# Two fill products between row and key scores in every step, and an earlier query fetch, in a kernel of attention and a Fourier layer

## The chip, the cores and the metric

One core of a Trainium2 chip. The metric is device time in microseconds for one execution, the median of several. Engines: PE is TensorE (PEld its weight loads), DVE VectorE, ACT ScalarE, POOL GpSimd, SP SyncE, which issues nearly all DMAs. PSUM holds what TensorE writes.

## The reference

Two independent layers whose outputs stand side by side; everything is fp32.

```
# A: attention, x [2048, 1024], 32 heads of 32, one k and v for all heads
q = x @ wq;  k = x @ wk;  v = x @ wv
p = softmax(q_h @ k.T * 32**-0.5)          # for each head h: 2048 x 2048
a = concat_h(p @ v) @ wo
# B: Fourier layer, xB [2048, 1024]
re = xB @ Wd_re.T;  im = xB @ Wd_im.T
b = Ws_re @ re - Ws_im @ im
out = concat([a, b], axis=-1)              # [2048, 2048]
```

## The kernel before

**Units and steps.** Attention is cut into 32 units: 4 blocks of 512 queries by 8 groups of four heads. A unit takes 32 steps (`SU`), and each step handles two different units at two stages. The first is a *row step* `score_step(s)`: `scores(s)` makes the scores of 128 queries by 1024 keys with two products into a PSUM tile `pss` (two buffers); VectorE takes the row maximum (`TENSOR_REDUCE nm<-pss`, 1024 of them); `row_sums(s)`, which is emitted one step later, lets ScalarE take the exponential in place and sum it. The sums and maxima give the log-sum of each row, which `lse_1` to `lse_4` write into two spare rows of the query tile `qst`. The second is a *key step* n = s - 52 (`SU + LEAD`): `key_scores(n)` makes the transposed scores of 128 keys by 1024 queries with two products into `pst` (one buffer of two PSUM banks), with the log-sum already subtracted, and `key_exp(n)` lets ScalarE take the exponential into an SBUF tile `p` (15 buffers).

**Bursts.** In steps 15 and 31 of a unit (`LASTS`) `pv` multiplies the exponentials of eight chunks of keys with v: 64 matmuls of 32 columns, four heads side by side, into a bank `psb`. This is the burst. `key_exp` of that step is emitted after its first chunk.

**Fills.** All other matmuls of the two layers (query and output projections and the Fourier layer, each fp32 product as three fp32r products of high and low parts, and with seven products for eight by Strassen's scheme) are a list of groups of 24 or 12 products, which accumulate in one of two PSUM banks (`ps_b`). `take(n)` emits the next n of them; I call them fills. `pos["fill"]` counts them, and a planner (`Line`, `pump`, `at`) issues loads, casts and stores by that count. When a group is complete, `post` reads its bank, on VectorE as a rule. There are 5328 fills ahead of the last groups, 408 of them before step 0.

**Spread of the fills.** `goal(n)` says how many fills should be done by step n; `level(n)` takes the rest up to the goal of the next burst, divided by the steps that are left, rounded. In a burst step it takes none, but `pv` first calls `aside`, which takes 0 to 5 fills so that the open group is at least six products old or complete. TensorE's order in a step was: row scores, key scores, then all fills of the step (or `aside`'s and the burst).

**Query tiles.** `qst` has three buffers. `open_unit(u + 1)` is emitted in row step 26 of unit u (`SU - 6`), six steps ahead of its first row scores: three DMAs from `qh_d` and `ql_d` and, from the fourth tile on, one that clears two rows. All go through SP's queue, in order with the other loads and stores.

Each engine runs its instructions in the order in which the program emits them. Nearly all instructions have one line in the profile (L79), since the class `Ordered` emits them; groups are told apart by their tiles: `pss<-kst,qst` is a row score, `pst<-qst,kst` a key score, `psb<-rh,mh` and the like a fill, `psb<-p,v` the burst.

Of the kernel before, what the change touches and what calls it, by code (L numbers as in the profile page):

```python
# [101 lines left out]
def tile_kernel(ctx: ExitStack, tc, xT, wq, wkv, wo, xbT, wT, cT, out):  # L102
# [51 lines left out]
    class Line:  # L154
# [24 lines left out]
        def pump(self):  # L179
            for k in range(4):  # L180
                while self.may(k) and self.items[self.n[k]].due - self.lead[k] <= pos["fill"]:
                    self.step(k)
# [94 lines left out]
    def add(gs):  # L277

        for g in gs:
            i0 = g.at = end[0]  # L280
            end[0] += g.n
            if groups and g.set[0] is not groups[-1].set[0]:
                prev["set"] = prev["this"]
                prev["this"] = i0
            for c, it in enumerate(g.right):
                if it.need is None:
                    it.need = i0 + 3 * c
                    p0 = min(prev["set"], i0 - it.back)
                    it.due = min(it.need, p0 + (i0 - p0) * (g.first + c + 1) // (len(g.set) * len(g.right))) - it.ahead
                    RL.items.append(it)  # L290
                it.last = i0 + 3 * c + 2
            for c, it in enumerate(g.left):
                if it.need is None:
                    it.need = it.due = i0 + 12 * c
                    ML.items.append(it)
                it.last = i0 + 12 * c + 11
            for it in g.ys:
                it.due = i0 + g.n
                ylist.append(it)
            groups.append(g)  # L300
# [14 lines left out]
    def at(p, f):  # L315
        k = len(later)
        while k and later[k - 1][0] > p:
            k -= 1
        later.insert(k, (p, f))

    def run_later():
        while later and later[0][0] <= pos["fill"]:
            later.pop(0)[1]()
# [29 lines left out]
    def bank(name, open_=False):  # L353

        while held:
            held.pop(0)()
        b = 1 - cur["bank"] if cur["bank"] is not None else int(used[1] < used[0])
        cur["at"] += 1
        used[b] = cur["at"]
        if open_:  # L360
            cur["bank"] = b
        return ps_b[b].tile([P, W], F32, name=name)
# [10 lines left out]
    def product(g, ps, j):  # L373
        c, w = divmod(j, 3)
        l, r = g.left[c // 4], g.right[c]
        a = (l.lo if w == 2 else l.hi)[:, c % 4]
        te.matmul(ps[:g.rows], a, r.lo if w == 1 else r.hi, start=j == 0, stop=j == g.n - 1)

    def take(n):
        for _ in range(n):  # L380
            if cur["group"] >= len(groups):
                return
            g = groups[cur["group"]]
            j = pos["fill"] - g.at
            if j == 0:
                cur["ps"] = bank("psb", True)
            if j % 3 == 0:
                RL.force(g.right[j // 3])
            if j % 12 == 0:
                ML.force(g.left[j // 12])  # L390
            product(g, cur["ps"], j)
            pos["fill"] += 1
            if j == g.n - 1:
                cur["group"] += 1
                assert all(hasattr(it, "done") for it in g.ys)
                g.post(cur["ps"])
                cur["at"] += 1
                used[cur["bank"]] = cur["at"]
                cur["bank"] = None
                if g.ys:  # L400
                    at(pos["fill"] + 2 * BEHIND + 5, lambda n=len(g.ys): yused.__setitem__(0, yused[0] + n))
            pump()
            run_later()
# [174 lines left out]
    def wo_set(e):  # L578
        return [Item([(lambda g=g: wo[g * P:(g + 1) * P, e * W:(e + 1) * W], 1)]) for g in range(NG)]
# [143 lines left out]
    units = [(b, g) for b in range(NQ) for g in range(NG)]  # L723
    SU = 32
# [5 lines left out]
    def open_unit(u):  # L730
        b, g = units[u]
        assert ("q", b, g) in ready
        if u < 3:
            rows.append(qsp.tile([P, 4, W], F32R, name=f"qst{u}"))
            gp.memset(rows[u][96:P].bitcast(F32), 0.0)
        q = rows[u % 3]
        if u >= 3:
            move(sp, q[96:98].rearrange("p a b -> p (a b)"), kst[98:100])
        for r, src in enumerate((qh_d, ql_d, qh_d)):
            move(sp, q[r * DH:(r + 1) * DH], src[b][g].rearrange("(h d) c -> d h c", d=DH))  # L740
        qst[u] = q
        nm[u] = sm.tile([P, 10, NC], F32, name="nm")

    def scores(s):
        u, r = divmod(s, SU)
        i, j = divmod(r, 2)
        h, t = divmod(i, 4)
        ps = ps_s.tile([P, 2 * W], F32, name="pss")
        for a in range(2):
            k0 = (2 * j + a) * W  # L750
            te.matmul(ps[:, a * W:(a + 1) * W], qst[u][:, h, t * P:(t + 1) * P], kst[:, k0:k0 + W], start=True, stop=True)
        dve.tensor_reduce(nm[u][:, j, i:i + 1], ps, axis=AX.X, op=ALU.max, negate=True)
        pend[s] = ps

    def row_sums(s):
        if s not in pend:
            return
        ps = pend.pop(s)
        u, r = divmod(s, SU)
        i, j = divmod(r, 2)  # L760
        act.activation(ps, ps, AF.Exp, bias=nm[u][:, j, i:i + 1], accum_out=nm[u][:, 8 + j, i:i + 1])
# [24 lines left out]
    def lse_3(u):  # L786
        pm = ps_s.tile([P, 2 * W], F32, name="pss")
        te.transpose(pm[:3 * NC, :P], nm[u][:, 3:6].rearrange("p a b -> p (a b)"), ident)
        mt = sm.tile([3 * NC, P], F32, name="mt")
        dve.tensor_copy(mt, pm[:3 * NC, :P])  # L790
        lse[u] = mt
# [7 lines left out]
    def inverse(u):  # L799
        rb[u] = onp.tile([P, W], F32, name="rb")  # L800
        for h in range(4):
            r = r_d[u][4 * h:4 * h + 4].rearrange("t c -> (t c)")
            sp.dma_start(rb[u][h * DH:(h + 1) * DH], r.unsqueeze(0).to_broadcast([DH, W]))

    def key_scores(n):
        u, r = divmod(n, SU)
        c, hp_ = divmod(r, 2)
        ps = ps_t.tile([P, 2, W], F32, name="pst")
        for a in range(2):
            te.matmul(ps[:, a], kst[:, c * P:(c + 1) * P], qst[u][:, 2 * hp_ + a], start=True, stop=True)  # L810
        return ps

    def key_exp(n, ps):
        u, r = divmod(n, SU)
        c, hp_ = divmod(r, 2)
        pt[u, c, hp_] = pp.tile([P, 2, W], F32, name="p")
        act.activation(pt[u, c, hp_], ps, AF.Exp)
# [49 lines left out]
    def score_step(s):  # L867

        if s < total:
            u, r = divmod(s, SU)  # L870
            if r == SU - 6 and u + 1 < len(units):
                open_unit(u + 1)
        if SU <= s < SU * (len(units) + 1) and s % SU == TURN:
            row_sums(s - 1)
            lse_3((s - SU) // SU)
        if s < total:
            scores(s)
        row_sums(s - 1)
        u, e = divmod(s - SU, SU)
        if 0 <= u < len(units):  # L880
            for f in LSE.get(e, ()):
                f(u)
# [37 lines left out]
    for s in range(SU + LEAD):  # L920
        score_step(s)
        take(6)
# [9 lines left out]
    def goal(n):  # L932
        return PRO + (FILL - PRO - LAST - MORE * (total - QUIET)) * n // total + MORE * max(n - QUIET, 0)


    def level(n):
        r = n % SU
        if r in LASTS:
            return
        more = min(e for e in LASTS if e > r) - r  # L940
        left = goal(n + more + 1) - pos["fill"]
        take(round(left / more))

    for n in range(total):
        u, r = divmod(n, SU)
        if n == total - 12:
            w1 = wo_set(1)
            add([o_group(NQ - 1, t, e, ws) for e, ws in ((0, w0), (1, w1)) for t in range(4)])
        score_step(n + SU + LEAD)
        if ends:  # L950
            ends.pop(0)()
        ps = key_scores(n)
        if r == 16:
            inverse(u)
        if r in LASTS:
            pv(u, LASTS.index(r), lambda: key_exp(n, ps))
        else:
            key_exp(n, ps)
        level(n)


    last = groups[len(groups) - 8:]
# [73 lines left out]
```

## Time and profile before

| | |
|---|---|
| median of 3 runs | 2704.43 us (2704.22 to 2705.95) |
| profiled execution, its own time | 2704.65 us |
| its span, first to last instruction | 2702.9 us |
| mean granted TensorE clock | 0.999 |
| PE busy | 2691.3 us, 13820 matmuls |
| ACT busy | 2128.3 us, 79% |
| POOL busy | 1736.4 us, 64% |
| DVE busy | 1569.6 us, 58% |

Matmuls are pipelined: one is shown with about 0.39 us, though the next starts sooner, so TensorE's pace is read from the distance of starts and not from busy time. A wait counts only where it makes a hole in the stream of the engine that sets the end.

### The profile page before, as it was taken

To read this page: it belongs to the slowest core of one execution; us is meant where nothing else is said; L and a number is where in the kernel's file an instruction comes from. 1 tells how busy PE (TensorE), PEld (TensorE's weight loads), DVE (VectorE), ACT (ScalarE), POOL (GpSimd) and SP (SyncE) were. 2 spreads that over 40 slices of the span, in tenths; PEclk is the share of its full clock that TensorE was granted. 3 is DMA by queue.
4 is the path that set the end of the run, shared out by engine and by line. 5 is a ranking of instruction groups with operands and counts; after the bars stand their busy time and mean duration, and the time that the engine had idled before them with its cause. 6 is when DMAs were issued, how large, how long until landed. Compare 5 with 4: busy or idle time off the path is not lost.

```text
span 2702.9 us, 40398 instructions
## 1 busy us (share of the span) xinstructions
PE 2691.3 (100%) x13820; PEld 1922.0 (71%) x13820; DVE 1569.6 (58%) x1794; ACT 2128.3 (79%) x3130; POOL 1736.4 (64%) x1712
## 2 busy tenths in 40 slices
PE   9999999999999999999999999999999999999999
PEld 6876776677667677677776776677677677667767
DVE  5866666666666666555655556665565556556300
ACT  3688888888888878888888887788898888788641
POOL 4754525777557548766556775566797898866741
PEclk9999999999999999999999999999999999999999
DMA  8543335887687565564444678874675666644565
GB/s 275 184 141 119 122 108 187 291 285 238 228 299 272 189 228 188 172 195 137 145 152 152 198 245 286 292 242 137 219 225 167 210 195 179 193 140 152 184 211 186
DMA packets 316930, 538.24 MB, mean 199 GB/s; under 512 B 35962, under 2 KB 63354, under 8 KB 316666
## 3 DMA queue, kind: packets, MB, share of 16 engines
q1 hardware_dynamic: 315572, 533.69, 61.1%
q8 instruction: 109, 1.79, 0.3%
q10 hardware_dynamic: 1152, 1.97, 0.2%
q14 instruction: 97, 0.79, 0.1%
HBM read 395.58 MB, written 138.15 MB: 197 GB/s over the span
## 4 chain that ended last, share of the span: by engine, by line
PE 68%; DMA 1%; issue 0%; ACT 0%; POOL 0%; DVE 0%; SPq 0%; POOLq 0%; DVEq 0%; ACTq 0%
PE psb L79 42%; PE pst L79 13%; PE pss L79 12%; DMA m<-o 1%; DMA y<-c 0%; DMA out_dram<-y 0%; DMA qst<-qh 0%; ACT pss L79 0%; ACT p L79 0%; DMA c<-y 0%; POOL ov L79 0%; POOL ml L79 0%; DVE nm L79 0%; SPq L79 0%; POOL m L79 0%
## 5 line engine op out<-in xcount | busy, mean ns | idle before, releaser
L79 DVE TENSOR_REDUCE nm<-pss 128x1 f32<-128x1024 f32 x1024 | 1252.4, 1223 | 530.3 <-PE pss L79 529.3
L79 ACT ACTIVATE p<-pst 128x1024 f32<-128x1024 f32 x1026 | 1059.1, 1032 | 451.3 <-PE pst L79 362.7
L79 ACT ACTIVATE pss<-pss,nm 128x1024 f32<-128x1024 f32 x1024 | 1118.0, 1092 | 55.7 <-DVE nm L79 54.2
L79 PE MATMUL psb<-rh,mh 128*128 128x512 f32 x1790 | 699.5, 391 | 0.1
L79 PE MATMUL psb<-rl,mh 128*128 128x512 f32 x1790 | 699.2, 391 | 0.0
L79 PE MATMUL psb<-rh,ml 128*128 128x512 f32 x1790 | 698.5, 390 | 0.0
L79 PE MATMUL pst<-qst,kst 128*128 128x512 f32 x2048 | 644.8, 396 | 1.2 <-ACT p L79 0.8
L79 PE MATMUL pss<-kst,qst 128*128 128x512 f32 x2048 | 638.9, 393 | 4.7 <-ACT pss L79 2.5
L79 POOL TENSOR_TENSOR ml<-m,mh 128x512 fp32r<-128x512 f32 x366 | 473.3, 1293 | 44.8 <-PE psb L79 22.2
L79 PEld LDWEIGHTS pss<-kst,qst 128*128 128x128 f32 x2048 | 380.0, 188 | 109.1 <-issue 26.3
L79 PE MATMUL psb<-p,v 128*32 128x512 f32 x4096 | 452.7, 594 | 0.4 <-DVE y L79 0.3
L79 PEld LDWEIGHTS pst<-qst,kst 128*128 128x128 f32 x2048 | 371.5, 188 | 111.6 <-ACT p L79 38.8
L79 POOL CAST mh<-m 128x512 fp32r<-128x512 f32 x366 | 224.9, 614 | 304.0 <-PE psb L79 273.7
L79 PEld LDWEIGHTS psb<-rh,mh 128*128 128x128 f32 x1790 | 336.6, 188 | 75.9 <-ACT rh L79 1.6
L79 PEld LDWEIGHTS psb<-rl,mh 128*128 128x128 f32 x1790 | 336.6, 188 | 72.8 <-DVE rl L79 1.0
L79 PEld LDWEIGHTS psb<-rh,ml 128*128 128x128 f32 x1790 | 336.6, 188 | 71.8
L79 PEld LDWEIGHTS psb<-p,v 128*32 128x32 f32 x4096 | 126.5, 110 | 291.4 <-issue 282.7
L79 POOL TENSOR_TENSOR m<-m,m 128x512 f32<-128x512 f32 x220 | 283.8, 1290 | 62.9 <-DMA m<-o 24.0
L79 POOL TENSOR_TENSOR rl<-r,rh 128x512 fp32r<-128x512 f32 x208 | 268.7, 1292 | 4.1
L79 ACT ACTIVATION_READ_ACCUMULATOR pss<-pss,nm 128x1 f32 x1024 | 216.2, 211 | 0.0
L79 POOL TENSOR_TENSOR ov<-ov,rb 128x512 f32<-128x512 f32 (+1 forms) x46 | 59.3, 1289 | 243.0 <-DVE ov L79 235.0
L79 POOL CAST rh<-r 128x512 fp32r<-128x512 f32 x208 | 127.6, 613 | 121.6 <-PE psb L79 61.5
(80 smaller groups left out, 859.1 us busy)
## 6 DMA issues: line engine op xcount, KB each, us to landing
m<-in_cT_dram SPq DMA_DIRECT2D x384, 256.0 KB
r<-s SPq DMA_DIRECT2D x192, 256.0 KB
y<-y SPq DMA_DIRECT2D x128, 256.0 KB
r<-in_wT_dram SPq DMA_DIRECT2D x88, 256.0 KB
m<-in_xbT_dram SPq DMA_DIRECT2D x88, 256.0 KB
y<-u SPq DMA_DIRECT2D x80, 256.0 KB
m<-in_wq_dram SPq DMA_DIRECT2D x64, 256.0 KB
qst<-qh SPq DMA_DIRECT2D x64, 256.0 KB
```

The source lines that it names most:

```text
L79: return lambda *a, **k: self.tc.keep_in_program_order(f(*a, **k))
```

## The change

1. Row step 22 of a unit (`SU - 10`) and no longer step 26 opens the next unit's query tile.
2. `level(n)` returns the number of fills of step n and no longer takes them; in a burst step it returns 2.
3. Up to two of these fills are taken between the row scores and the key scores, the others where all of them were before.

```
-            if r == SU - 6 and u + 1 < len(units):
+            if r == SU - 10 and u + 1 < len(units):
                 open_unit(u + 1)
...
     def level(n):
         r = n % SU
         if r in LASTS:
-            return
+            return 2
         more = min(e for e in LASTS if e > r) - r
         left = goal(n + more + 1) - pos["fill"]
-        take(round(left / more))
+        return max(round(left / more), 0)
...
         score_step(n + SU + LEAD)
         if ends:
             ends.pop(0)()
+        fill = level(n)
+        first = min(fill, 2)
+        take(first)
         ps = key_scores(n)
         if r == 16:
             inverse(u)
         if r in LASTS:
             pv(u, LASTS.index(r), lambda: key_exp(n, ps))
         else:
             key_exp(n, ps)
-        level(n)
+        take(fill - first)
```

## Rows read from the trace of the kernel before

**Rows 1.** The page, part 1: busy us (share of the span) xinstructions of each engine
```profile
PE 2691.3 (100%) x13820; PEld 1922.0 (71%) x13820; DVE 1569.6 (58%) x1794; ACT 2128.3 (79%) x3130; POOL 1736.4 (64%) x1712
```

**Rows 2.** Timeline of a step with five fills: start us, us, engine, line, operation, tiles
```profile
1215.53 1.08 ACT L79 ACTIVATE pss<-pss,nm 128x1024 f32<-128x1024 f32 x1
1215.53 0.62 PE L79 MATMUL pss<-kst,qst 128*128 128x512 f32 x2
...
1215.99 0.61 PE L79 MATMUL pst<-qst,kst 128*128 128x512 f32 x2
1216.19 1.23 DVE L79 TENSOR_REDUCE nm<-pss 128x1 f32<-128x1024 f32 x1 [0.81 <-PE pss L79]
...
1216.64 1.03 ACT L79 ACTIVATE p<-pst 128x1024 f32<-128x1024 f32 x1
...
1217.35 0.41 PEld L79 LDWEIGHTS pss<-kst,qst 128*128 128x128 f32 x2
1217.56 1.08 ACT L79 ACTIVATE pss<-pss,nm 128x1024 f32<-128x1024 f32 x1
1217.57 0.62 PE L79 MATMUL pss<-kst,qst 128*128 128x512 f32 x2
```

**Rows 3.** Busy time by stretch, steps 1 to 14 after a burst; columns as printed
```profile
core 0: us, PE busy (x) PEld busy (x) DVE busy (x) ACT busy (x) POOL busy (x), PEclk, DMA share, GB/s
1246.33:1275.11 28.78, 28.78 (x128) 23.84 (x127) 19.47 (x23) 28.78 (x44) 21.12 (x23) 1.00 0.60 183
1168.68:1197.14 28.46, 28.46 (x126) 23.38 (x125) 19.59 (x23) 28.46 (x44) 27.05 (x28) 1.00 0.74 235
1325.21:1353.59 28.38, 28.38 (x124) 22.83 (x123) 19.17 (x23) 28.38 (x44) 18.66 (x20) 1.00 0.65 197
...
2350.57:2378.84 28.27, 28.27 (x122) 22.19 (x121) 19.13 (x23) 28.27 (x45) 25.96 (x26) 1.00 0.69 207
1285.32:1314.12 28.80, 28.80 (x128) 23.84 (x127) 18.95 (x18) 28.63 (x44) 18.72 (x20) 1.00 0.36 119
2389.53:2417.92 28.39, 28.39 (x126) 23.38 (x125) 18.99 (x17) 28.38 (x43) 21.25 (x21) 1.00 0.36 123
656.32:684.58 28.26, 28.26 (x124) 22.82 (x123) 20.72 (x20) 28.24 (x43) 17.82 (x19) 1.00 0.84 278
```

**Rows 4.** Timeline of steps with four and five fills in turn
```profile
995.19 1.02 ACT L79 ACTIVATE p<-pst 128x1024 f32<-128x1024 f32 x1
996.10 1.10 ACT L79 ACTIVATE pss<-pss,nm 128x1024 f32<-128x1024 f32 x1
...
997.18 1.05 ACT L79 ACTIVATE p<-pst 128x1024 f32<-128x1024 f32 x1
998.09 1.12 ACT L79 ACTIVATE pss<-pss,nm 128x1024 f32<-128x1024 f32 x1
...
996.64 1.22 DVE L79 TENSOR_REDUCE nm<-pss 128x1 f32<-128x1024 f32 x1 [0.28 <-PE pss L79]
...
998.28 0.73 PE L79 MATMUL pst<-qst,kst 128*128 128x512 f32 x2
...
998.28 0.30 PEld L79 LDWEIGHTS pst<-qst,kst 128*128 128x128 f32 x2 [0.26 <-ACT p L79]
```

**Rows 5.** Chain of waits, its longest pieces: start us, us, what (two of 46 bursts)
```profile
1041.87 7.00 PE psb L79 x64
...
1001.07 8.14 PE psb L79 x69
```

**Rows 6.** Timeline of TensorE at the end, when no row scores are left
```profile
2594.92 0.70 PE L79 MATMUL pst<-qst,kst 128*128 128x512 f32 x2
...
2596.82 0.70 PE L79 MATMUL pst<-qst,kst 128*128 128x512 f32 x2
```

**Rows 7.** Timelines of SP and of TensorE at the first row scores of a unit
```profile
1029.43 0.43 SPq L79 DMA_DIRECT2D qst<-qh  x1
...
1034.66 0.70 PE L79 MATMUL pss<-kst,qst 128*128 128x512 f32 x2 [1.12 <-DMA qst<-qh]
```

**Rows 8.** Timeline of ScalarE in the first unit
```profile
164.01 1.09 ACT L79 ACTIVATE pss<-pss,nm 128x1024 f32<-128x1024 f32 x1 [0.24 <-DVE nm L79]
```

More of the change, by code (lines that the diff above doesn't have):

```diff
@@ L870, in score_step @@
             u, r = divmod(s, SU)
-            if r == SU - 6 and u + 1 < len(units):
+            if r == SU - 10 and u + 1 < len(units):
                 open_unit(u + 1)
@@ L938, in level @@
         if r in LASTS:
-            return
+            return 2
         more = min(e for e in LASTS if e > r) - r
         left = goal(n + more + 1) - pos["fill"]
-        take(round(left / more))
+        return max(round(left / more), 0)
     for n in range(total):
@@ L951, in tile_kernel @@
             ends.pop(0)()
+        fill = level(n)
+        first = min(fill, 2)
+        take(first)
         ps = key_scores(n)
@@ L958, in tile_kernel @@
             key_exp(n, ps)
-        level(n)
+        take(fill - first)
     last = groups[len(groups) - 8:]
```

## The prediction

> **What bounds the kernel now.** I first read the page: TensorE is busy for nearly all of the span, ScalarE for 79% of it [rows 1]. Nothing is gained by a shorter VectorE or GpSimd step as long as TensorE's stream has no holes, so the question is where it has holes, and which engine makes them. The timeline of an ordinary step [rows 2] answers what a step is. Two row products start at 1215.53, two key products at 1215.99, the next row products at 1217.57: four scores and five fill products in 2.04 us, that is 0.227 us each (2.04/9). In the same step ScalarE makes one exponential of a row tile (1.08 us) and one of a key tile (1.03 us); starts repeat after 2.03 us (1215.53, 1217.56). So five fills are just enough for ScalarE, and a step of four fills lasts only 8 x 0.227 = 1.82 us.
>
> The timeline of a stretch with fours shows the limit [rows 4]: key exponentials start at 995.19 and 997.18, row exponentials at 996.10 and 998.09, each 1.99 us apart and back to back. This is ScalarE's pace when it has everything: 1.99 us a step. The weights of the next key product wait 0.26 us for ScalarE there, because the key scores have one tile in PSUM, which is free only when its exponential ends, and the pair starts 0.34 us apart instead of 0.227 (0.73 us for two, against 0.61).
>
> The decisive view is busy time by stretch, steps 1 to 14 after a burst, each with another number of fill products [rows 3]. The count of TensorE's instructions is 56 scores, the fills, and one that reaches in. ScalarE is busy in all of the stretch or all but 0.17 us of it, so its 79% is an average over these stretches and the bursts. And the time follows the fills no longer: after the second burst of a unit (first four rows) 128, 126, 124 and 122 instructions take 28.78, 28.46, 28.38 and 28.27 us. Two products are worth 0.454 us of TensorE, but taking two away saves 0.32, then 0.08, then 0.11 us. After the first burst (last three rows) it is 0.41 and 0.13 us. Below 126, ScalarE sets the time.
>
> **The change, part by part.** Removed: nothing; every product, exponential and DMA stays. Moved are fills, key scores and the query fetch.
>
> *Two fills in each burst step.* The rule that spreads the fills asks for 75.9 in sixteen steps ((5328 - 408 - 12 - 52)/1024 x 16). Before, the burst step only tidies up a group: 0 to 5 fills, seen as bursts of 64 to 69 instructions in the chain of waits [rows 5]. So the other fifteen steps get 76 less what the burst before took. Following the rule through the group lengths (24 and 12), the 60 full stretches ahead of the end have 76 fills 23 times, 75 seven times, 70 to 74 thirty times; steps of four come to 79. After the change, the burst step takes two more, and the fifteen get 74 less that number: 74 fills 23 times, 73 eight times, 68 to 72 28 times, 75 once; steps of four come to 169. Each stretch loses two products and the burst, where ScalarE has little to do, is 0.454 us longer. What this costs is 0.454 less what the stretch saves: from 76, 0.09 (mean of 0.13 and 0.04, from 0.32 and 0.41); from 74 or less, 0.35 (savings of 0.08 to 0.13); from 75 the mean of the two, 0.22. Sum: 23 x 0.09 + 7 x 0.22 + 30 x 0.35 = 14.1 us. Bounds: 10 if the saving per pair were 0.2 us, 18 if stretches below 70, which no row shows, saved nothing at all.
>
> The Trainium skill (Perfetto Trace Analysis, Optimization Strategy) says that where the most-contended engine differs between regimes, interleaving the regimes may help. That speaks against this edit: a burst is the regime of TensorE alone, and more of TensorE's work is put into it; the sum above would keep its sign by it.
>
> *Key scores behind two fills.* A key pair now starts 0.908 us after the row pair instead of 0.454. The distance from one key pair to the next is unchanged (two fills leave the end of the step and come ahead of the pair), so the wait of key scores for ScalarE keeps its slack. Two others change. The row exponential comes after the key exponential in ScalarE's order, so it starts 0.454 later against its row products: the maximum that it needs ends at 1217.42 (1216.19 + 1.23) and it starts at 1217.56, a slack of 0.14 us that becomes 0.59. Where VectorE is late, as in the wait of 0.24 us at 164.01 [rows 8], up to 0.45 us an event is forgiven. Such places are the ends of query groups (24 fills each, so about 16 in the first 80 steps, and VectorE reads each result twice), at 0.11 us of TensorE for the widened pair and at most as much again for a late start, and late DMAs at up to 0.45 us. 16 x 0.22 and three late DMAs make 5 us, the bound; the other is 0, and I take the half, -2.5 us, since not every group ends right ahead of row scores. The other change is against it: a row tile (two of them) is free 0.454 later. It ends now 3.11 us after its products began (1217.56 + 1.08 less 1215.53); then 3.56, while the products two steps on load weights at 4.08 - 0.22 = 3.86 us (weights at 1217.35 for products at 1217.57 [rows 2]). That still holds, by 0.3 us; I cost it at nothing. With that cover gone, in two steps of 3.86 us in sum (a five and a four), it would be 3.64 against 3.56 and the wait up to 0.1 us on about 90 additional fours: 0 to 6 us.
>
> *The end.* Once no row scores are left, steps of two key products and six fills take 1.90 us (2594.92 to 2596.82) and not 8 x 0.227 = 1.82: the one key tile bounds them [rows 6]. The three last stretches hold eight fills fewer by the rule (92, 88, 92 become 86, 88, 90); where the key tile bounds, these save nothing. At most 8 x 0.227 = 1.8 us, at least 0; I take 1.2, as most of the steps there are bound so.
>
> *Query tiles four steps sooner.* The same four DMAs (three for the first tiles) move by four steps, 8.2 us, ahead of other loads in SP's queue; none is added. They wait for key products of a unit that ended two steps and a burst earlier, so nothing behind them in SP's queue is held. In the whole trace one fetch was late: its last DMA was issued at 1029.43 and the row products waited 1.12 us at 1034.66 [rows 7]. That goes: -1.1 us. Loads that it passes are up to four issues later, some 2 us by their spacing on SP; I take nothing for that. Bounds 0 (another load is late) and -1.4 (with the wider pair behind it).
>
> Sum against the profiled execution's own 2704.65 us (span 2702.9): 14.1 - 2.5 + 1.2 - 1.1 = +11.7, so 2716.4; the median of the runs shown is 0.2 lower. I forecast **2716 us**.
>
> **The rivals.** *ScalarE has room, no change (0.22).* The page of the profile gives it 79%. The Trainium skill (Perfetto Trace Analysis, Identifying the Most-Contended Engine) calls occupancy a fair measure of how near ScalarE is to its limit; by that 21% are free, and the longer bursts would be paid back between them. In rows: the pair ahead of the key scores lets the exponentials run denser than 1.99 us, so the fifteen steps save nearly all of the 0.454 us. Then the fetch and some VectorE lateness are left, 2704.65 - 1.1 - 1.5 = 2702, and with half of the payback 2709. Against it: ScalarE's 28.46 of 28.46 us [rows 3].
>
> *VectorE made the holes, faster (0.18).* If the row exponential waits for VectorE's maximum in the steps of four, the 0.454 us of new room ends these waits. Holes behind fours are now 79 x about 0.13 = 10 us (28.27 us for 122 against 121 x 0.227 = 27.47, so 0.80 for five fours; less for the first); without them and with the other gains in full: 2704.65 - 10 - 2.5 - 1.1 = 2691, and half of it 2698. It decides from the point where the maximum ends later than the row exponential could start. Against it: in the stretch with fours the maximum ends at 997.86 (996.64 + 1.22) and the exponential starts at 998.09, right behind the key exponential [rows 4].
>
> *Row tiles become the wait (0.10).* The 0 to 6 us above fall due, and with the upper bound of the moved fills: 2704.65 + 18 + 6 - 1 = 2728.
>
> **How the numbers follow.** The forecast itself has 0.50, range 2708 to 2725 (10 + 0 - 1.4 - 5 = +3.6; 18 + 1.8 = +19.8). The range for 8 in 10 reaches into both neighbours: 2700 to 2726, and leaves out the faster end of the second rival and most of the third. A measurement here tells 0.2% (5.4 us) from no change: slower is above 2709.8. The forecast gives 0.47 of its 0.50 to slower, the third rival 0.10 and the first 0.03: 0.60. Faster (below 2699): most of the second, some of the first, 0.17. The rest, 0.23, is the same.
>
> **What would show it.** Burst steps' time between row scores up by 0.45 us; nearly all stretches with 74 fills or less, and the steps around fours at 1.99 us; weights of key products waiting for ScalarE about twice as often; ScalarE still 100% between bursts. The wait for a query tile gone. Wrong would be: stretches of 124 instructions well under 28.3 us (ScalarE faster than I read), or row products waiting for ScalarE often (third rival).

## The result

The changed kernel takes 2709.12 us (median of 21 runs, 2707.91 to 2711.06); the kernel before took 2704.34 us beside it. The ratio is 1.0018, 95% interval 1.0011 to 1.0025: 4.9 us slower. The forecast was 11.7 us slower; the direction held, the size did not. The time lies near the lower end of the stated range (2708 to 2725), and under the line above which the prediction would call it slower (2709.8).

Page of the changed kernel, parts 1 and 4 (busy time by engine; then the chain that ended last, by engine):
```profile
PE 2700.0 (100%) x13820; PEld 1903.8 (70%) x13820; DVE 1570.4 (58%) x1794; ACT 2120.9 (78%) x3130; POOL 1736.5 (64%) x1712
...
PE 99%; DVE 0%; ACT 0%; DMA 0%; issue 0%; SPq 0%
```
The averages are within a point of those of [rows 1]. The chain runs through TensorE for 99% of the span. The same line of the page before:
```profile
PE 68%; DMA 1%; issue 0%; ACT 0%; POOL 0%; DVE 0%; SPq 0%; POOLq 0%; DVEq 0%; ACTq 0%
```
These two can't be compared as they stand: before, the chain could be followed back only to 804.90 us, so it covers 70% of the span, and 68 of these 70% are TensorE's. Of the rest most lies between 1706 and 1790 us, in DMAs and GpSimd; after the change the chain has no such piece there. That is the first sign that something besides the spread of the fills changed.

Busy time by stretch of the changed kernel, the same stretches and columns as in [rows 3] (the last row is a stretch with 69 fills, of which there was none):
```profile
1248.90:1277.37 28.47, 28.47 (x126) 23.31 (x125) 19.67 (x23) 28.47 (x44) 21.70 (x23) 1.00 0.57 176
1170.65:1199.13 28.48, 28.48 (x126) 23.31 (x125) 19.58 (x23) 28.48 (x44) 27.70 (x27) 1.00 0.79 241
1327.58:1355.95 28.37, 28.37 (x124) 22.59 (x123) 19.08 (x22) 28.37 (x44) 18.62 (x20) 1.00 0.66 201
...
2353.32:2381.58 28.26, 28.26 (x122) 21.94 (x121) 19.03 (x22) 28.26 (x44) 25.94 (x25) 1.00 0.64 196
1288.07:1316.44 28.37, 28.37 (x126) 23.30 (x125) 19.02 (x18) 28.37 (x43) 19.21 (x20) 1.00 0.37 122
...
656.54:684.81 28.27, 28.27 (x124) 22.62 (x123) 20.73 (x21) 28.27 (x43) 18.44 (x18) 1.00 0.83 279
2274.47:2302.67 28.20, 28.20 (x121) 21.59 (x120) 19.00 (x22) 28.20 (x44) 27.35 (x28) 1.00 0.74 233
```
Read the first row against the first of [rows 3]: two products fewer (126 for 128) save 0.31 us and not 0.454; its fifth row saves 0.43. And 126, 124, 122 and 121 instructions take 28.47, 28.37, 28.26 and 28.20 us, with ScalarE busy in all of it: ScalarE's pace, as the forecast had it, and within 0.02 us of what the same number of products took before.

Timeline of ScalarE and of weight loads in a stretch with fours:
```profile
942.47 1.10 ACT L79 ACTIVATE pss<-pss,nm 128x1024 f32<-128x1024 f32 x1
...
944.46 1.11 ACT L79 ACTIVATE pss<-pss,nm 128x1024 f32<-128x1024 f32 x1
...
946.46 1.13 ACT L79 ACTIVATE pss<-pss,nm 128x1024 f32<-128x1024 f32 x1
...
943.74 0.30 PEld L79 LDWEIGHTS pss<-kst,qst 128*128 128x128 f32 x2 [0.26 <-ACT pss L79]
```
Row exponentials start 1.99 to 2.00 us apart, as in [rows 4]. But now the row products wait for ScalarE as well. The waits of the whole execution (us in total, times, longest), before and after:
```profile
PEld pst L79 <- ACT p L79: 38.8, 146, 0.7
PEld pss L79 <- ACT pss L79: 4.4, 5, 2.1
```
```profile
PEld pst L79 <- ACT p L79: 40.9, 205, 0.6
PEld pss L79 <- ACT pss L79: 29.6, 114, 0.4
```
The additional holes lie at the row tile (5 to 114 times), not at the key tile as I had written. It costs nothing more: whichever product waits, the step is as long as ScalarE's two exponentials, as the equal times for equal counts above show. Row products that wait for ScalarE often were a sign of being wrong in the prediction's own list; it came up, without the price that the third rival gave it.

What the forecast missed is in the stretches that were not ScalarE's. Busy time of four stretches (steps 1 to 14 after a burst: the first of all, the one of the late query tile, and two next to each other), before:
```profile
142.73:172.05 29.32, 29.23 (x127) 23.34 (x126) 20.77 (x25) 28.61 (x44) 17.40 (x18) 1.00 0.53 171
1011.31:1040.78 29.47, 28.35 (x123) 22.54 (x122) 20.20 (x24) 28.50 (x44) 28.27 (x29) 1.00 0.67 206
1717.10:1749.29 32.19, 30.18 (x126) 24.08 (x125) 22.52 (x30) 29.73 (x45) 19.35 (x20) 0.96 0.96 317
1760.83:1791.44 30.61, 29.47 (x124) 22.41 (x123) 23.84 (x27) 28.52 (x43) 24.64 (x26) 1.00 0.92 304
```
and after:
```profile
143.41:172.04 28.63, 28.63 (x127) 23.63 (x126) 20.75 (x25) 28.61 (x44) 17.77 (x19) 1.00 0.53 167
1012.67:1040.98 28.31, 28.31 (x123) 22.27 (x122) 20.18 (x24) 28.31 (x44) 27.84 (x29) 1.00 0.70 214
1723.02:1751.14 28.12, 28.12 (x120) 21.21 (x119) 21.30 (x26) 28.12 (x44) 18.16 (x19) 1.00 0.91 319
1762.27:1790.87 28.60, 28.60 (x124) 22.51 (x123) 23.23 (x27) 28.39 (x43) 24.92 (x26) 1.00 0.86 280
```
These four alone gave back 0.69 + 1.16 + 4.07 + 2.01 = 7.9 us; about 0.3 of it is for the six products that the third lost. The forecast had 3.6 us for the whole kernel. The chain of waits from 1700 to 1800 us says what held the two long ones, before and after (shares by line):
```profile
by line: PE psb L79 29.9%; DMA m<-o 13.6%; issue 9.8%; PE pst L79 7.6%; PE pss L79 6.7%; DMA y<-c 6.0%; DMA out_dram<-y 5.9%; DMA c<-y 3.3%; POOL ov L79 2.6%; POOL ml L79 2.6%; DVE nm L79 2.5%; ACT pss L79 2.4%; ACT p L79 1.8%; POOL m L79 1
```
```profile
by line: PE psb L79 61.9%; PE pss L79 19.4%; PE pst L79 17.8%; DVE qh L79 0.7%; DVE y L79 0.6%; issue 0.1%
```
There the output projection's products start: their left sides are attention outputs, read back from memory (`m<-o`), and their partial sums go out and come back (`c<-y`, `y<-c`). Before, TensorE waited for these loads through VectorE and ScalarE; after, it waits for none.

### The profile page after: what moved, and what is told of

The parts are those of the page before. It is cut to its first block, busy times and chain, and to the rows that moved or that the text cites. A ratio compares the mean times of both kernels' runs of the same rounds, so it can differ in the third digit from the quotient of the medians.

```text
span 2707.2 us, 40395 instructions
## 1 busy us (share of the span) xinstructions
PE 2700.0 (100%) x13820; PEld 1903.8 (70%) x13820; DVE 1570.4 (58%) x1794; ACT 2120.9 (78%) x3130; POOL 1736.5 (64%) x1712
## 4 chain that ended last, share of the span: by engine, by line
PE 99%; DVE 0%; ACT 0%; DMA 0%; issue 0%; SPq 0%
PE psb L79 62%; PE pss L79 20%; PE pst L79 18%; DMA m<-in_wq_dram 0%; DVE qh L79 0%; DVE nm L79 0%; ACT p L79 0%; DVE y L79 0%; ACT pss L79 0%; ACT mh L79 0%; ACT rh L79 0%; DVE p L79 0%; SPq L79 0%; DVE mt L79 0%
## 5 line engine op out<-in xcount | busy, mean ns | idle before, releaser
L79 PE MATMUL pss<-kst,qst 128*128 128x512 f32 x2048 | 650.7, 399 | 0.9 <-DVE mt L79 0.9
L79 PEld LDWEIGHTS pss<-kst,qst 128*128 128x128 f32 x2048 | 366.5, 188 | 128.8 <-ACT pss L79 29.6
L79 PEld LDWEIGHTS pst<-qst,kst 128*128 128x128 f32 x2048 | 367.6, 188 | 109.1 <-ACT p L79 40.9
L79 ACT ACTIVATION_READ_ACCUMULATOR pss<-pss,nm 128x1 f32 x1024 | 224.7, 219 | 0.0
```

What stands on the lines that cost most here:

```text
L79: return lambda *a, **k: self.tc.keep_in_program_order(f(*a, **k))
```

## Experiments

Each is timed beside the kernel before (medians of 2705.0 to 2705.4 us). Theory A: the burst fills cost what the steps of four say, and what came back came back because VectorE's lateness does no harm in the new order. Rivals: the burst fills cost less than summed (B); the fetch re-timed SP's queue (C).

**The three parts, one by one and together.** Fetch alone:
```
-            if r == SU - 6 and u + 1 < len(units):
+            if r == SU - 10 and u + 1 < len(units):
```


> Only the query fetch is four steps sooner; order and fills as before. Theory A (the fills in burst steps cost about 14 us as summed, and the pair ahead of the key scores gave back some 9 us by making late VectorE work harmless): only the one late fetch goes, 1.1 to 1.4 us less than before, about 2703. Theory C (the holes went because the fetch re-timed SP's queue): 6 to 9 us less, 2695 to 2698, and the holes of steps 653 to 670 are gone.

Pair alone is the changed kernel with `SU - 6` and with `return 0` for `return 2`.


> Only the pair between row and key scores of ordinary steps; none in burst steps; fetch as before. A: the spread of the fills is that of before (76 less what the burst took), so steps of four cost the 10 us that they cost before, and the holes behind late VectorE work shrink by 6 to 9 us: 2695 to 2698. Theory B (the fills cost only 5 us and the pair gives nothing): 2703 to 2705. C: 2704.

Burst fills alone: the changed kernel with `SU - 6` and
```
-        first = min(fill, 2)
+        first = min(fill, 2) if r in LASTS else 0
```


> Only the two fills in burst steps, ahead of their key scores; ordinary steps in the old order; fetch as before. A: plus 13 to 15 us, 2717 to 2719, with 169 steps of four and ScalarE busy in all of the stretches. B: plus 4 to 6 us, 2709 to 2710.

The three combinations of two, made from the same lines:


> The pair in ordinary steps and the earlier fetch, no fills in burst steps (the changed kernel less its burst fills). A: 1 us under the pair alone, 2694 to 2697, and so better than both kernels. B: 2703. C: 2695 to 2698 as well, but then the fetch alone gives the same.

> The changed kernel with the old, later query fetch. Theory A (the three parts give about what their own runs show: two burst fills +9, the pair's order some -8 where the burst step has its own two fills, the fetch -4 to -5): 2712 to 2714. Theory B (the fetch gains only what waits for a query tile, 1.1 us): 2710.

> The two fills in burst steps and the earlier fetch, ordinary steps in the old order (the eighth of the eight combinations). Theory A (the parts add up: the steps of four cost what their number says, and the other holes, some 12 us before, are ended by 3 us by the fetch and by 6 to 9 us by the order): 2711 to 2713, and the holes of the first 80 steps stay. Rival (the fetch alone cures the other holes): 2709, as the changed kernel.

| burst fills | pair | fetch | median us | ratio to before, 95% interval |
|---|---|---|---|---|
| no | no | yes | 2700.11 | 0.9981 (0.9973 to 0.9990) |
| no | yes | no | 2719.11 | 1.0052 (1.0038 to 1.0066) |
| no | yes | yes | 2715.51 | 1.0037 (1.0024 to 1.0049) |
| yes | no | no | 2714.64 | 1.0034 (1.0022 to 1.0047) |
| yes | no | yes | 2712.70 | 1.0027 (1.0016 to 1.0038) |
| yes | yes | no | 2711.80 | 1.0022 (1.0013 to 1.0031) |
| yes | yes | yes | 2709.12 | 1.0018 (1.0011 to 1.0025) |

In us (ratio less one, times 2705) from before: fetch -5.1; pair +14.1; burst fills +9.2; the changed kernel +4.9. An interval is some 2 to 4 us on either side: each part alone is clear of it, the differences among the four rows with burst fills are not. Of the six expectations only the one for burst fills with fetch was met as theory A said; that for pair with burst fills was missed by 0.2 us, the other four by more, and each miss says something. A table by stretch in the next section takes the time of each kernel apart.

*The fetch gains 5.1 us alone and 1 to 2 us beside the burst fills* by these ratios; that the two differ is not clear of the intervals. It gains more than the one late tile (1.1 us): in its trace the stretch with the output projection is 29.44 us (1715.66 to 1745.10) instead of 32.19. Of these 2.75 us some 1.2 are a low clock behind the hole of before (last section), which this trace does not have. SP's timeline shows how the rest can come about. Before:
```profile
1728.19 0.63 SPq L79 DMA_DIRECT2D qst<-kst  x1
...
1730.72 0.30 SPq L79 DMA_DIRECT2D qst<-qh  x1
1731.42 1.62 SPq L79 DMA_DIRECT2D m<-o  x2
1734.15 0.32 SPq L79 DMA_DIRECT2D c<-y  x1
```
With the earlier fetch:
```profile
1720.31 0.63 SPq L79 DMA_DIRECT2D qst<-kst  x1
...
1721.89 0.43 SPq L79 DMA_DIRECT2D qst<-qh  x1
...
1730.33 0.91 SPq L79 DMA_DIRECT2D m<-o  x2
1731.63 0.32 SPq L79 DMA_DIRECT2D c<-y  x1
```
The four fetch DMAs occupied SP just ahead of the loads that were late; earlier, they stand among other loads. `c<-y` goes out 2.5 us sooner; 1.4 of this is that the stretch itself begins sooner, so 1.1 us are gained on it, while `m<-o` gains nothing. The next stretch became 0.4 us longer (31.05), so the fetch in part moved these waits. Theory C holds for a part at most: its 6 to 9 us did not come, and by which load the gain came is not shown.

*The pair without burst fills is the worst of all.* My expectation overlooked the seam. If the pair stands ahead of the key scores in step 14 but not in the burst step, only three fills and two row products lie between the two key pairs. Timeline of weight loads in this kernel, key products of steps 14 and 15:
```profile
1200.52 0.30 PEld L79 LDWEIGHTS pst<-qst,kst 128*128 128x128 f32 x2 [0.27 <-ACT p L79]
...
1202.52 0.30 PEld L79 LDWEIGHTS pst<-qst,kst 128*128 128x128 f32 x2 [0.55 <-ACT p L79]
```
These are 2.00 us apart for seven products, which take 1.59: 0.41 us lost at this burst. At the 62 of 64 bursts with seven products between the pairs the distance is 1.73 to 2.01 us, and the 60 bursts of the table below take 19.3 us longer than before, 0.32 each. What the expectation was about happened: the holes of the stretches fall from 12.3 to 3.9 us, and A had 6 to 9 less. Hence the fills in burst steps too: the two there cost bursts 0.454 us and spare most of the seam. With them the pair gains 2.4 to 3.2 us (2712.70 to 2709.12 by the ratios' difference 0.0009, 2714.64 to 2711.80 by 0.0012); neither difference is clear of the intervals.

*The burst fills alone cost 9.2 us, not 13 to 15; beside the earlier fetch 12.4* (7.3 + 5.1). The moved fills cost what they should: in the trace of the burst-fill kernel the 60 bursts are 25.8 us longer and the stretches, by their counts, 11.8 us shorter, 14.0 us in all. That is theory A's price and not B's. But its stretch with the output projection takes 28.39 us (1728.98 to 1757.37) where it was 32.19, so a lengthening can hide behind a wait that is there anyway; why the loads came in time there was not tested. The late query tile got worse: its hole grew from 1.2 to 3.5 us.

**ScalarE's pace.** Half of each row exponential is left out, in both kernels:
```
-        act.activation(ps, ps, AF.Exp, bias=...
+        act.activation(ps[:, :W], ps[:, :W], AF.Exp, bias=...
```


> The kernel before with the row exponential over half of its columns only (the other half of the row sums is left out), so ScalarE has about 0.4 us less to do in a step. Theory A (ScalarE's 1.99 us sets the steps of four): the waits of the steps of four go, 10 to 13 us less than before, about 2693. Rival (the one key tile, or the row tiles, set them): less than 4 us.

> The changed kernel with the same half exponential. A: the 169 steps of four cost no more than the 79 did, so the changed kernel is no longer the slower one: 2688 to 2692, 0 to 4 us under the half-exponential kernel before. Rival: still 4 to 6 us above it.

2694.76 us (0.9964, 0.9952 to 0.9977) and 2691.05 us (0.9948, 0.9935 to 0.9960). Both are as theory A said. With ScalarE relieved the changed kernel is 3.7 us the faster one (its five runs, up to 2691.3, all lie below the other's five, from 2692.3), though it has the same 169 steps of four: what they cost is for the most part ScalarE's time. Stretches of 134 and 132 products take 30.55 and 30.21 us there (15 steps, as in the table below), so two products less save 0.34 of 0.454 us; in the changed kernel it is 30.57 for both. What keeps it from 0.454 was not tested; key products still wait for ScalarE (43.3 us, 219 times, against 40.9 and 205), so such waits alone are no measure of cost. ScalarE now waits in nearly every step (over 0.05 us ahead of 1022 of 1026 key exponentials; 175 in the changed kernel), as here:
```profile
934.17 1.03 ACT L79 ACTIVATE p<-pst 128x1024 f32<-128x1024 f32 x1 [0.15 <-PE pst L79]
935.10 0.66 ACT L79 ACTIVATE pss<-pss,nm 128x512 f32<-128x512 f32 x1
```

**VectorE's lateness.** The maximum is taken over half of each row, the other half left out, in both kernels:
```
-        dve.tensor_reduce(nm[u][:, j, i:i + 1], ps, ...
+        dve.tensor_reduce(nm[u][:, j, i:i + 1], ps[:, :W], ...
```


> The kernel before with VectorE's maximum over half of the columns (the other half of each row is left out of it), 0.5 us less on VectorE in every step, the order as before. Theory A (the order of the changed kernel ended holes that VectorE makes by being late for the row exponential): the same holes end without a change of order, the ones of the first 80 steps above all: 3 to 8 us less than before, 2697 to 2702. Rival (the order helps in another way): within 1 us of before.

> The changed kernel with the same half maximum. A: nothing is left there for a faster VectorE to end, within 1.5 us of the changed kernel, 2708 to 2710. Rival: 3 us less or more, as in the kernel before.

2699.63 us (0.9980, 0.9971 to 0.9989) and 2707.14 us (1.0007, 0.9998 to 1.0016): 5.4 us for the old order, about 3 us (1.0018 less 1.0007) for the new one. A says 3 to 8 and at most 1.5: the first is met, the second is not. In the traces the holes of the stretches fall by 5.2 us in the old order (12.3 to 7.1) and by 0.4 in the new one; there the bursts are 1.1 us shorter. So the new order leaves next to no hole for a faster VectorE to end, as A has it, but not all of what the faster maximum gives is such a hole. Waits of ScalarE and of the key products in the first 80 steps (141 to 345 us), before:
```profile
ACT pss L79 <- DVE nm L79: 4.1, 14, 0.6
PEld pst L79 <- ACT p L79: 4.1, 13, 0.5
```
after the change:
```profile
PEld pst L79 <- ACT p L79: 1.1, 6, 0.3
ACT pss L79 <- DVE nm L79: 0.6, 1, 0.6
```
and in the kernel before with half the maximum:
```profile
ACT pss L79 <- DVE nm L79: 0.6, 1, 0.6
PEld pst L79 <- ACT p L79: 0.4, 2, 0.3
```
Fourteen late exponentials become one, by a change of order or by a faster maximum alike, and the 2.8 us of holes of the first five stretches go with either. There theory A is shown.

**Fewer fills in bursts.** If fills in a burst are what costs, the tidying should shrink (and not grow):
```
+        m = 6 if held else 3
-        if 0 < j < 6:
-            take(6 - j)
-        elif j > g.n - 6:
+        if 0 < j < m:
+            take(m - j)
+        elif j > g.n - m:
             take(g.n - j)
```
It was run on the fetch alone, on the changed kernel, and on a form with one fill for two (`min(fill, 1)`, `return 1`), which was run with the old tidying too.


> The earlier fetch alone, and the burst step tidies up less: a group need be only three products old or three from its end (six as before where a second reading of the other bank is still due). So a burst takes fewer fills and the stretch behind it more. A: steps of four become rare, 6 to 9 us less than with the fetch alone, 2691 to 2694. Rival: bursts wait for the reading of their bank, 0.3 us or more in every second one, and eat this up: 2699 to 2703.

> The changed kernel with the smaller tidying of the run before (three products instead of six). A: most stretches have 74 fills, one four each at 0.02 to 0.11 us, so the stretches lose some 5 us instead of 23: 2690 to 2692. Rival (the fours do not set it): 2703 or more.

> The changed kernel with one fill in place of two, between the scores and in burst steps. A: fours fall to about 116, 7 us less in the stretches, and 0.23 us of room for VectorE ends most other holes: 2701 to 2703. Rival (0.23 us is too little room, half of the holes come back): 2706 to 2708.

> The one-fill form with the smaller tidying. A: hardly any fours and little of the other holes left: 2684 to 2688, the fastest of all. Rival (0.23 us is too little room): 2690 to 2692, as with the two-fill form.

2691.95 us (0.9951, 0.9937 to 0.9964), 2695.56 (0.9963, 0.9950 to 0.9977), 2702.58 (0.9992, 0.9983 to 1.0001) and 2690.33 (0.9947, 0.9934 to 0.9959). All four go the way of A: each is faster than the same kernel with the old tidying or with two fills. The first and the third are as A said; the second and the last lie 3.6 and 2.3 us above it. The last is where its rival had it (2690 to 2692, as the two-fill form), but the two-fill form took 2695.56, so that rival's reason did not hold either; what kept the second and the last from A's figures was not looked into. The first and the last beat the kernel before by 13 to 14 us, the changed kernel by more, and are not told apart. In the first, waits of key products for ScalarE fall by half, from 38.8 us and 146 times:
```profile
PEld pst L79 <- ACT p L79: 20.4, 77, 0.6
```

## Why the prediction was wrong in size

The traces allow the whole account, for one execution of each kernel. A stretch is taken here from the first row product of the step behind a burst to that of the next burst step (15 steps), the burst from there to the first row product of the step behind it; 60 of each lie ahead of the end. "By count" prices every stretch at the median of the stretches, of the kernels before and after, that have as many products (136 take 30.96 us, 134 30.60, 132 30.57, 130 30.44). The four columns behind it are what the stretches take above that price: their holes. All in us:

| kernel | stretches by count | first five | late query tile (from 1009) | output projection (two, from 1715) | other 52 | bursts |
|---|---|---|---|---|---|---|
| before | 1843.2 | 2.8 | 1.2 | 6.0 | 2.3 | 507.7 |
| fetch | 1843.2 | 2.8 | 0.1 | 3.7 | 2.2 | 507.1 |
| pair | 1843.2 | -0.1 | 1.5 | 2.7 | -0.2 | 527.0 |
| pair, fetch | 1843.2 | -0.1 | 0.0 | 1.6 | -0.3 | 526.9 |
| burst fills | 1831.4 | 2.8 | 3.5 | 1.5 | 1.1 | 533.6 |
| burst fills, fetch | 1831.4 | 2.9 | 0.1 | 1.7 | 1.0 | 533.4 |
| burst fills, pair | 1831.4 | 0.2 | 1.3 | 0.2 | 1.0 | 535.0 |
| changed (all three) | 1831.4 | 0.2 | 0.0 | 0.2 | -0.9 | 535.1 |
| before, half maximum | 1843.2 | -0.1 | 2.5 | 2.8 | 1.9 | 506.8 |
| changed, half maximum | 1831.4 | -0.1 | 0.0 | 0.2 | -1.1 | 534.0 |

From before to the changed kernel, bursts take 27.35 us more (0.456 each) and stretches by their counts 11.8 less: the moved fills cost 15.5 us. Holes fall from 12.3 to -0.5, 12.8 us less. With 0.7 us more ahead of step 0 and 0.9 more at the end, that is the 4.3 us between the spans (2702.9 and 2707.2).

- *ScalarE sets the stretches between bursts*: right. 28.47 of 28.47 us busy after the change, 1.99 us a step, and the half exponential turns the sign. The Trainium skill (Perfetto Trace Analysis, Identifying the Most-Contended Engine) calls ScalarE's occupancy a fair measure of how close it is to its limit, and 78% would leave room. The trace does not agree (28.47 of 28.47 us in a stretch), since an average over bursts and stretches hides an engine that is full in the one and has waits in the other.
- *Each pair of fills moved into a burst costs 0.09 to 0.35 us, 14.1 in all*: right, at 15.5 us, inside the bounds of 10 and 18. The burst step grew by 0.456 us, as forecast.
- *What comes back, -2.5 for VectorE and late DMAs and -1.1 for the late fetch*: this step failed. The sum took the stretches as set by TensorE or ScalarE and gave 3.6 us for everything else; 12.8 us came back. The term that was too small above all is "late DMAs at up to 0.45 us", three of them: two stretches from 1715 to 1799 us, held by loads of the output projection, had 6.0 us of holes, 1.2 of them a low clock behind one hole (last section), and no row was from there. The trace of the kernel before had the sign: twelve of its 60 stretches take 0.3 to 3.8 us longer than others with as many products.
- *The pair gives room for VectorE (-2.5, bound -5)*: right in kind; that its size fits beside the burst fills (2.4 to 3.2 us) is in part luck. In the traces it ends 6.1 us of holes there, more than the bound, and gives back 1.4 to 1.7 us in the bursts and 0.7 to 1.1 at the end. The first five stretches show it cleanly: 2.8 us with the old order, 0.2 or less with the new one, whatever the fetch and the burst fills are.
- *The fetch (-1.1, bound -1.4)*: right for the late tile (its hole goes from 1.2 to 0.1 us), too small as a whole: -5.1 alone, and 2.6 to 3.5 us of holes in each of the four pairs of traces that differ in it alone. The loads that the fetch passes were taken at nothing, and those behind its old place were not looked at: the output projection's holes fall from 6.0 to 3.7 us, the low clock's 1.2 among them.
- *Terms as a sum*: at the output projection the three parts end the same 6.0 us, by 2.3 (fetch), 3.3 (pair) and 4.5 (burst fills) alone, which would be 10 together. What is ended once can't be ended twice, so their prices depend on which are there already.
- *Row tiles hold, at nothing*: wrong as a fact (114 waits, for 5), right in price: the changed kernel's stretches take no longer than others with as many products.
- *The end*: steps without row scores still take 1.90 us after the change (key products at 2593.85 and 2595.75). From the first row product of row step 1012 on, the changed kernel takes 0.9 us longer than before, burst fills alone 0.2, the pair alone 1.9: the loss there goes with the order, which the forecast had at nothing, and hardly with the eight fills that it had at 1.2.
- *The range*: that the time lies in it is in part luck. Its lower end was made of a cost of 10 us and gains of 6.4; measured are 15.5 and 12.8.

Open is why the burst fills end most of the holes at the output projection (6.0 to 1.5 us), and why the late query tile differs so much between kernels (1.2 to 3.5 us where the fetch is late); in the kernel before with half the maximum a second one was late.

## What to carry to other kernels

An engine at 79% can be the limit in most of the stretches: take its busy time by stretch, and see whether the stretch gets shorter when other work is taken out of it. If not, don't move work out of it into a place where that engine idles. And before adding terms over all repeats, compare repeats with the same work: those that take longer than the others are held by something else, and there a cost can hide and a gain be larger than its cause. Check, too, how far back a chain of waits reaches before reading its shares.

## What the runs showed of the hardware

A hole in TensorE's stream cost more than itself. In the kernel before, row products started 1.71 us late at 1745.38 and key products another 0.30 us at 1746.41. Busy time just behind (PEclk is the third column from the end):
```profile
1746.73:1750.14 3.41, 3.41 (x9) 2.64 (x8) 2.75 (x9) 2.80 (x5) 0.61 (x2) 0.50 1.04 396
```
For 3.41 us the granted clock is 0.50, the level of 1.2 GHz, and products start 0.43 us apart instead of 0.227. By these two distances that is 1.6 us on top of the holes. The kernel with burst fills alone fell to 0.50 as well, at 1040.15, behind row products that started 1.85 us late at 1038.98. The changed kernel has no such place before its end, so part of what came back is this. It goes with the times: in the four groups of runs beside the experiments, those of the kernel before with a mean clock of 0.999 lie at 2705.6 to 2706.1 us in the mean, those with 1.000 at 2703.4 to 2705.2.
